# Four projection chunks in one run: moving PSUM users and matmul groups in a fused attention and MoE kernel

## The chip, the cores and the metric

The kernel runs on one core of one Trainium2 chip. The metric is the time of one execution on the device in microseconds; lower is better. Times of a kernel are given as the median of its runs. PE is the tensor engine, PEld its weight loads, DVE the vector engine, ACT the scalar engine, POOL the GpSimd engine, and SP the engine that starts most of the transfers.

## The reference

Eight batches (B = 8) of eight heads, 512 tokens of 64 elements and 32 state rows each. Cross attention goes both ways, and the result of all heads, 512 wide, goes through a two-layer block with an exact Gelu.

```python
scores = scale * np.matmul(x, state.transpose(0, 1, 3, 2))    # softmax over the state rows -> a
xread = np.matmul(a, state)
scores2 = scale * np.matmul(state, x.transpose(0, 1, 3, 2))   # softmax over the tokens -> a2
sread = np.matmul(a2, x)
y = np.concatenate([xread, sread], axis=2)                    # (B, H, 512 + 32, 64)
x = y.transpose(0, 2, 1, 3).reshape(B * 544, 512)
h = x @ w_in                                                  # 512 x 2048
g = 0.5 * h * (1.0 + erf(h / sqrt(2)))
return g @ w_out                                              # 2048 x 512
```

## The kernel before

**The work of a batch.** `scores` (L325) multiplies the transposed tokens with the state and takes the exponential on ACT; `norm` (L347) divides by the row sums on DVE; `atr_dma` (L378) transposes the result into AT by a transfer. The product of attention and first layer is folded: `p_mm` (L423) multiplies the state of a batch with w_in into P, in four chunks f = 0 to 3 of 512 columns. Each chunk is eight matmuls on 64-row, 32-column parts of the PE array, and fills two PSUM banks; `p_copy` (L438) takes the first bank out on ACT and the second on DVE. `mm1` (L489) then makes hidden chunk m of 16 as P times AT, two matmuls of 512 columns into one bank (hp), and ACT's Gelu empties the bank into g. M(k, k + 1) in the text is such a pair of hidden chunks.

**The second layer** goes as seven products of half-size blocks rather than eight, called X with a name "1" to "7" (L621), sixteen matmuls of 256 columns each. Their operands are sums of blocks of g, which `g_sum` (L582) makes on DVE, and of w_out (`w_sums`). X writes one of four fixed banks, o0 to o3: "3" and "5" use o0, "4" and "2" o1, "1" and "7" o2, "6" o3. After "3" ACT copies the bank to s3 (L635); after "4" DVE makes s34 (L640); after "5" ACT copies (L643) and POOL makes u (L646); after "1" DVE makes q (L652); after "2" ACT copies (L648), POOL makes v (L610) and DVE adds v to o3 (L618); after "7" DVE adds u (L654) and SP starts an output transfer.

**The reads.** `sread` (L386) multiplies the exponentials with the tokens on 32-column parts of the array, into one bank; `sread_out` (L400) divides on DVE straight from that bank into srm. `srt` (L413) transposes srm on PE, through another bank, and DVE copies it to XSR (L419).

**PSUM.** There are eight banks: the four fixed ones above, which `otile` gives, and four that `ftile` gives in rotation to scores, hidden chunks, P chunks, reads and srT. A user of a rotating bank waits until the user four before it has been emptied.

**The order** of work on each engine is the program's order, written by hand; no scheduler moves it. The main loop (L1116) has a slot for each batch b from 2 to 7, of eight parts p. A slot runs all hidden chunks of batch b, the X of batch b - 1 (parts 0 to 4) and the X "3" and "6" of batch b, and prepares batch b + 1 (nb): scores in part 1, norms in parts 2 and 3, the transfer of AT in part 5. `p_run` (L898) makes P of nb in two runs of two chunks: in part 5, chunks 0 and 1, after the reads; in part 7, chunks 2 and 3, after the M pair and before X "6". In slot 2, `pmat` (L1142) makes chunks 2 and 3 of batch 2 itself, one each in parts 0 and 3. In slot 6 the reads of batches 6 and 7 are made together. Slot 7 has another body (`read_out_slot`, L923).

Of the kernel before, what the change touches and what calls it, by code (L numbers as in the profile page):

```python
# [9 lines left out]
FP32 = mybir.dt.float32  # L10
BF16 = mybir.dt.bfloat16
# [6 lines left out]
def kernel(  # L18
# [36 lines left out]
    def otile(shape, name, at=None):  # L55
        if at is None:
            at = turn[0] % 4
            turn[0] += 1
        return ps_o.tile(shape, FP32, name=name, tag=f"o{at}")

    def ftile(shape, name):
        return ps_f.tile(shape, FP32, name=name, tag="f")
# [323 lines left out]
    def sread(b):  # L386
        A = atts[b]
        A.sr = ftile([128, 2, 65], "sr")
        for t in range(2):
            for j in range(SJ):  # L390
                for c in range(HC):
                    nc.tensor.matmul(  # L392
                        A.sr[32 * c:32 * c + 32, t, :],
                        lhsT=A.e[:, 2 * j + t, 32 * c:32 * c + 32],
                        rhs=A.xo[:, j, c, 1 + 65 * t:66 + 65 * t],
                        start=(j == 0),
                        stop=(j == SJ - 1),
                    )

    def sread_out(b):  # L400
        A = atts[b]
        A.srm = att.tile([128, 2, D], BF16, name="srm", tag="srm")
        flat = A.sr.rearrange("q t d -> q (t d)")
        inv = att.tile([128, 2], FP32, name="inv", tag="inv")
        nc.vector.reciprocal(out=inv, in_=flat[:, 0:130:129])
        nc.vector.tensor_tensor(
            out=A.srm,
            in0=flat[:, 1:129].rearrange("q (t d) -> q t d", t=2),
            in1=inv[:, :].to_broadcast((128, 2, D)),
            op=ALU.mult,  # L410
        )
# [11 lines left out]
    def p_mm(b, f, tiles):  # L423
        if b not in Ps:
            Ps[b] = att.tile([128, 2, d_ff], BF16, name="P", tag="P")
        ps = [tiles([128, 512], "p_ps") for t in range(2)]
        for c in range(HC):
            for t in range(2):
                nc.tensor.matmul(  # L429
                    ps[t][32 * c:32 * c + 32, :],  # L430
                    lhsT=sbd[64 * t:64 * t + 64, b, c, 32 * t:32 * t + 32],
                    rhs=w_in_bf[64 * t:64 * t + 64, c, f * 512:(f + 1) * 512],
                    start=True,
                    stop=True,
                )
        return ps

    def p_copy(b, f, ps):  # L438
        dst = Ps[b][:, :, f * 512:(f + 1) * 512]
        nc.scalar.copy(out=dst[:, 0, :], in_=ps[0])  # L440
        nc.vector.tensor_copy(out=dst[:, 1, :], in_=ps[1])  # L441

    def pmat(b, f):
        p_copy(b, f, p_mm(b, f, ftile))
# [137 lines left out]
    def g_sum(b, name):  # L582
        (h0, k0), (h1, k1), op = G_SUMS[name]
        t = apool.tile([128, MH, 256], BF16, name="gsum", tag="gsum")
        nc.vector.tensor_tensor(out=t, in0=g_q(b, h0, k0), in1=g_q(b, h1, k1), op=op)  # L585
        xs[b, "g" + name] = t
# [34 lines left out]
    def X(b, name):  # L621
        bank = {"3": 0, "4": 1, "5": 0, "2": 1, "1": 2, "6": 3, "7": 2}[name]
        first = name in "3416"
        if first:
            xs[b, bank] = otile([128, 2, NH], "xp", bank)
        ps = xs[b, bank]
        lhs = {"3": (0, 0), "4": (1, 1)}.get(name)
        lhs = xs[b, "g" + name] if lhs is None else g_q(b, *lhs)
        rhs = {"5": w_q[1][1], "2": w_q[0][0]}.get(name)
        rhs = w_sum[name] if rhs is None else rhs  # L630
        x_mm(ps, lhs, rhs, first)
        if name == "3":
            xs[b, "s3"] = c_tile("s3")
            if b > 1:
                nc.scalar.copy(out=xs[b, "s3"], in_=ps)  # L635
            for h in range(2):
                xs[b, "o", h] = hpool.tile([128, 2, d_model], FP32, name="oh", tag=f"oh{h}")
        elif name == "4":
            xs[b, "s34"] = c_tile("s34")
            nc.vector.tensor_tensor(out=xs[b, "s34"], in0=ps, in1=xs[b, "s3"], op=ALU.add)  # L640
        elif name == "5":
            o = xs[b, "o", 0][:, :, NH:]
            nc.scalar.copy(out=o, in_=ps)  # L643
            xs[b, "u"] = c_tile("u")
            x_out(b, 0, right)
            nc.gpsimd.tensor_tensor(out=xs[b, "u"], in0=xs[b, "s34"], in1=o, op=ALU.subtract)  # L646
        elif name == "2":
            nc.scalar.copy(out=xs[b, "o", 1][:, :, :NH], in_=ps)  # L648
            c22(b)
        elif name == "1":  # L650
            xs[b, "q"] = c_tile("q")
            nc.vector.tensor_tensor(out=xs[b, "q"], in0=ps, in1=xs[b, "s34"], op=ALU.add)  # L652
        elif name == "7":
            nc.vector.tensor_tensor(  # L654
                out=xs[b, "o", 0][:, :, :NH], in0=ps, in1=xs[b, "u"], op=ALU.add
            )
            x_out(b, 0, left)
# [77 lines left out]
    sr = {}  # L735
# [159 lines left out]
            nc.vector.tensor_tensor(out=rs["o", 0][:, :NH], in0=ps, in1=rs["u"], op=add)  # L895
            r_out(0)

    def p_run(b, fs, banks, copy=None):  # L898
        done = []
        for f, at in zip(fs, banks):  # L900
            it = iter(at or ())
            tiles = (lambda shape, name: otile(shape, name, next(it))) if at else ftile
            done.append((b, f, p_mm(b, f, tiles)))
        for x in done:
            (copy or p_copy)(*x)

    def p_copy_v(b, f, ps):
        for t in range(2):
# [6 lines left out]
    def M(*ms):  # L915
        for m in ms:
            mm1(m // MC, m % MC)
# [198 lines left out]
    for b in range(2, B):  # L1116
        nb = b + 1
        for p in range(8):
            k = 16 * b + 2 * p
            if p == 1 and nb < B:  # L1120
                scores(nb, 0)
                scores(nb, 1)
            if p in (2, 3) and nb < B:
                norm(nb, p - 2)
            if p == 3 and nb + 1 < B:
                xtr_dma(nb + 1)
            if p == 5 and nb < B:
                atr_dma(nb)
            if p == 7 and nb < B:
                srt(b)  # L1130
                if nb == B - 1:
                    srt(nb)
            if nb == B and p < 5:
                read_out_slot(p)
                if p == 4:
                    r_homes()
                    r_sum("5")
                    r_sum("2")
                continue
            M(k, k + 1)  # L1140
            if b == 2 and p in (0, 3):
                pmat(2, 2 + p // 3)  # L1142
            if b == 2 and p == 1:
                w_sums(4)
            if p < 5:
                if p == 0:
                    g_sum(b - 1, "5")
                    if b > 2:
                        sr_w("5216"[b - 3])
                X(b - 1, "45127"[p])  # L1150
                if p < 3:
                    g_sum(b - 1, "127"[p])
            if p == 0 and b + 3 < B:
                hold_for(b, 0)
                load_x(4 if b == 2 else b + 3)
            if p == 6 and b == 2:
                hold_for(b, 12)
                load_x(5)
            if p == 0 and nb + 1 < B:
                begin(nb + 1)  # L1160
                rearr(nb + 1)
            if nb == B:
                if p == 5:
                    g_sum(b, "6")
                    R("3")
                    r_sum("1")
                    R("4")
                    r_sum("6")
                    r_sum("7")
                if p == 6:  # L1170
                    R("5")
                    X(b, "3")
                    R("2")
                    R("1")
                if p == 7:
                    R("6")
                    X(b, "6")
                continue
            if p == 5:
                g_sum(b, "6")  # L1180
                reads = (b, nb) if nb == B - 1 else (b,)
                for r in reads:
                    sread(r)
                p_run(nb, (0, 1), ((0, 1), (3, 2)))
                for r in reads:
                    sread_out(r)
                if b == 2:
                    rearr_ones(3)
                elif nb + 1 < B:
                    rearr_ones(nb + 1)  # L1190
            if p == 6:
                X(b, "3")
            if p == 7:
                if b == 2:
                    rearr_ones(4)
                p_run(nb, (2, 3), ((1, 2), None))
                X(b, "6")
    b = B - 1
    for name in "521":
# [39 lines left out]
```

## Time and profile before

| | |
|---|---|
| median of three runs | 203.81 us (203.44 to 204.97) |
| span of the profiled execution | 202.5 us; the page gives no other time of that execution |
| what lies between the span and the runs | 0.9 us to the fastest, 1.3 us to the median |
| slot 2 (first M at 50.85) | 22.24 us |
| slots 3, 4, 5 (first M at 73.09, 94.43, 115.77) | 21.34 us each |
| slot 6 (first M at 137.10, the next slot's at 159.09) | 21.99 us |

The page comes from one execution. Its first part gives the busy time of each engine; matmuls are pipelined, so their durations overlap and the difference of two starts tells what PE spends on a group. A view of the waits says which engine sat idle before which instruction and what ended that. The timeline has one row for each group of like instructions: start, microseconds, engine, line, operation, output and inputs, shape and count, and in square brackets the idle time ahead of it and its releaser.

### The profile page before, as it was taken

How to read it: one execution, taken by the hardware profiler on the slowest of the kernel's cores; microseconds unless marked ns; L12 is line 12 of the kernel's file. 1: busy time of each engine (PE TensorE's matmuls, PEld its weight loads, DVE VectorE, ACT ScalarE, POOL GpSimd, SP SyncE). 2: the span in 40 equal slices, each digit the busy share in tenths (PEclk: the TensorE clock that was granted, in tenths of full speed). 3: DMA queues.
4: the chain of work that ended last, by engine and by line, in shares of the span. 5: the costliest groups of instructions: out<-in, count | busy, mean ns of one | idle time of the engine just before them, and what ended most of it. 6: DMA issues, size and time to landing. Idle time of an engine off the chain costs nothing.

```text
span 202.5 us, 4900 instructions
## 1 busy us (share of the span) xinstructions
PE 196.6 (97%) x2035; PEld 132.6 (65%) x2035; DVE 157.1 (78%) x255; ACT 135.4 (67%) x240; POOL 67.9 (34%) x75
## 2 busy tenths in 40 slices
PE   7898999999999999999999999999999999999994
PEld 2433544465667577766776687567775787878893
DVE  2953776789998979878897787768778988895882
ACT  3785577699885779566967596687847576864120
POOL 8962603323249555360627502430220002200000
PEclk9999999999999999999999999999999999999999
DMA  6999999977675788782774308440107001040125
GB/s 203 174 174 203 205 199 197 181 134 142 96 135 107 207 104 108 155 179 32 90 163 142 77 0 123 130 119 0 52 9 202 3 0 55 0 159 0 52 102 162
DMA packets 40566, 23.16 MB, mean 114 GB/s; under 512 B 21856, under 2 KB 39136, under 8 KB 40544
## 3 DMA queue, kind: packets, MB, share of 16 engines
q0 software_dynamic: 13984, 8.10, 29.3%
q1 hardware_dynamic: 25872, 14.36, 28.5%
q10 hardware_dynamic: 688, 0.39, 0.6%
q8 instruction: 16, 0.26, 0.5%
q14 instruction: 6, 0.05, 0.1%
HBM read 17.30 MB, written 8.91 MB: 129 GB/s over the span
## 4 chain that ended last, share of the span: by engine, by line
PE 89%; DMA 5%; POOL 4%; DVE 0%; issue 0%; POOLq 0%
PE xp L591 41%; PE hp L494 26%; DMA xb<-in_x_dram 5%; PE p_ps L429 4%; PE op L536 4%; PE sp L798 3%; PE rp L864 3%; POOL w_in_bf L105 2%; PE op L520 2%; PE xp L703 2%; PE pt L333 2%; PE sr L392 1%; POOL sbd L95 1%; POOL w_out_bf L113 1%; PE xT_ps L271 1%; POOL st_bf L121 0%
## 5 line engine op out<-in xcount | busy, mean ns | idle before, releaser
L501 ACT ACTIVATE g<-hp 128x512 bf16<-128x512 f32 x124 | 67.1, 605 | 27.9 <-PE hp L494 21.3
L494 PE MATMUL hp<-AT,P 128*128 128x512 bf16 x248 | 62.9, 379 | 0.0
L591 PEld LDWEIGHTS <-gsum 128*128 128x128 bf16 x528 | 51.0, 98 | 12.1 <-issue 1.9
L585 DVE TENSOR_TENSOR gsum<-g 128x2048 bf16<-128x2048 bf16 x35 | 45.5, 1314 | 0.1
L591 PE MATMUL xp<-ws,gsum 128*128 128x256 bf16 x304 | 36.3, 273 | 0.0
L494 PEld LDWEIGHTS <-P 128*128 128x128 bf16 x248 | 22.8, 98 | 20.5 <-issue 2.7
L591 PE MATMUL xp<-ws,g 128*128 128x256 bf16 x224 | 26.8, 273 | 0.0
L591 PE MATMUL xp<-w_out_bf,gsum 128*128 128x256 bf16 x224 | 26.6, 273 | 0.0
L591 PEld LDWEIGHTS <-g 128*128 128x128 bf16 x224 | 21.7, 98 | 4.6 <-issue 0.2
L646 POOL TENSOR_TENSOR u<-s,oh 128x512 f32<-128x512 f32 x6 | 8.8, 1466 | 41.1 <-ACT oh L643 41.1
L441 DVE CAST P<-p_ps 128x512 bf16<-128x512 f32 x29 | 18.7, 683 | 3.1 <-PE p_ps L429 2.9
L440 ACT CAST P<-p_ps 128x512 bf16<-128x512 f32 x29 | 15.8, 599 | 5.4 <-PE p_ps L429 5.1
L225 POOL COPY x<-xb 128x1024 bf16<-128x1024 bf16 x12 | 12.6, 1080 | 15.7 <-DMA xb<-in_x_dram 15.7
L235 POOL COPY xo<-xb 128x1024 bf16<-128x1024 bf16 x12 | 14.5, 1234 | 4.6 <-PE sr L392 4.6
L610 POOL TENSOR_TENSOR v<-q,oh 128x512 f32<-128x512 f32 x6 | 8.6, 1434 | 20.6 <-ACT oh L648 20.5
L536 PE MATMUL op<-w_out_bf,g 128*128 128x512 bf16 x48 | 11.8, 380 | 0.0
L356 DVE TENSOR_TENSOR a<-e,ics 128x512 bf16<-128x512 bf16 x14 | 10.7, 764 | 0.5
L429 PE MATMUL p_ps<-w_in_bf,sbd 64*32 64x512 bf16 x248 | 10.5, 382 | 0.0
L353 DVE TENSOR_REDUCE cs<-e 128x16 f32<-128x512 bf16 x14 | 9.5, 677 | 0.7 <-ACT e L340 0.7
L419 DVE COPY XSR<-srT 128x128 bf16<-128x128 bf16 x8 | 5.7, 759 | 5.5 <-PE srT L416 5.5
L501 ACT ACT_TABLE_LOAD x7 | 9.0, 1283 | 0.1
L618 DVE TENSOR_TENSOR oh<-xp,v 128x512 f32<-128x512 f32 x6 | 4.1, 690 | 5.2 <-POOL v L610 5.2
(132 smaller groups left out, 230.2 us busy)
## 6 DMA issues: line engine op xcount, KB each, us to landing
out_dram<-oh SPq DMA_DIRECT2D x15, 256.0 KB, 2.9
xb<-in_x_dram POOLq DMA_DIRECT2D x7, 512.0 KB, 5.9
out_dram<-oh SPq DMA_DIRECT2D x6, 512.0 KB, 2.9
w_in_bf<-in_moe_w_in_dram POOLq DMA_DIRECT2D x6, 256.0 KB, 12.4
out_dram<-osb SPq DMA_DIRECT2D x5, 256.0 KB, 3.2
w_out_bf<-in_moe_w_out_dram POOLq DMA_DIRECT2D x4, 256.0 KB, 8.9
w_out_bf<-in_moe_w_out_dram POOLq DMA_DIRECT2D x2, 512.0 KB, 13.3
x0f<-in_x_dram SPq DMA_DIRECT2D x3, 256.0 KB, 3.7
```

The lines of the kernel that those rows point to most:

```text
L225: nc.gpsimd.tensor_copy(out=A.x4[:, :, :, 64 * t:64 * t + 64].rearrange("p j c d -> p c j d"), in_=src[:, t],)
L235: eng.tensor_copy(out=A.xo[:, :, :, 2 + 64 * t:66 + 64 * t].rearrange("p j c d -> p c j d"), in_=src[:, t],)
L353: nc.vector.reduce_sum(out=cs, in_=e4, axis=AX.X)
L356: nc.vector.tensor_tensor(out=A.a[:, :, hs].rearrange("p g (c n) -> p g c n", n=NS), in0=e4, in1=ics[:, :, :].to_broadcast((128, G, 2, NS) ...
L429: nc.tensor.matmul(ps[t][32 * c:32 * c + 32, :], lhsT=sbd[64 * t:64 * t + 64, b, c, 32 * t:32 * t + 32], rhs=w_in_bf[64 * t:64 * t + 64, c ...
L440: nc.scalar.copy(out=dst[:, 0, :], in_=ps[0])
L441: nc.vector.tensor_copy(out=dst[:, 1, :], in_=ps[1])
L494: nc.tensor.matmul(hp, lhsT=Ps[b][:, t, m * 128:(m + 1) * 128], rhs=atts[b].AT[:, :, t, :], start=(t == 0), stop=(t == 1),)
L501: nc.scalar.activation(out=gs[b][:, m, :], in_=hp, func=AF.Gelu)
L536: nc.tensor.matmul(ops[b, j], lhsT=gs[b][:, m, j * 128:(j + 1) * 128], rhs=w_out_bf[:, m, :], start=(m == 0), stop=(m == MC - 1),)
L585: nc.vector.tensor_tensor(out=t, in0=g_q(b, h0, k0), in1=g_q(b, h1, k1), op=op)
L591: nc.tensor.matmul(ps[:, j - js[0], :], lhsT=lhs[:, m, 128 * j:128 * j + 128], rhs=rhs[:, m, :], start=(first and j == js[0] and m == 0), ...
```

## The change

In slots 2 to 6 the two runs of two chunks become one run of four in part 5. The run's banks are o0 and a rotating one for chunk 0, two rotating ones for chunk 1, o1 and o3 for chunk 2, o2 and a rotating one for chunk 3. The reads go ahead of it into one rotating bank; ACT copies them to the new tile sraw, and the division (on DVE, after the run's copies) reads sraw. X "7" of batch b - 1 moves from part 4 to part 5, ahead of the reads; X "3" of batch b moves from part 6 to part 5, right behind the run; g_sum "6" moves from part 5 to part 3. Part 4 is left with its M pair alone, part 6 too. In slot 2, chunks 2 and 3 of batch 2 are made as one pair from four rotating banks, in part 2 ahead of X "1", and that part's M pair now follows X "1".

```diff
-    def p_run(b, fs, banks, copy=None):
+    def reads_mm(bs):
+        sr = ftile([128, len(bs), 2, 65], "sr")
...
+        raw = cpool.tile([128, len(bs), 130], FP32, name="sraw", tag="sraw")
+        nc.scalar.copy(out=raw, in_=sr.rearrange("q i t d -> q i (t d)"))
+        return raw
+
+    def reads_norm(bs, raw):
...
+            nc.vector.reciprocal(out=inv, in_=raw[:, i, 0:130:129])
+            nc.vector.tensor_tensor(
+                out=A.srm,
+                in0=raw[:, i, 1:129].rearrange("q (t d) -> q t d", t=2),
+                in1=inv[:, :].to_broadcast((128, 2, D)),
+                op=ALU.mult,
+            )
+
+    def p_all(b, bs):
+        raw = reads_mm(bs)
         done = []
-        for f, at in zip(fs, banks):
...
+        for f, at in enumerate(((0, None), (None, None), (1, 3), (2, None))):
+            it = iter(at)
+
+            def tiles(shape, name):
+                i = next(it)
+                return ftile(shape, name) if i is None else otile(shape, name, i)
+
             done.append((b, f, p_mm(b, f, tiles)))
         for x in done:
-            (copy or p_copy)(*x)
+            p_copy(*x)
+        reads_norm(bs, raw)
+
+    def pmat_pair(b):
+        done = [(b, f, p_mm(b, f, ftile)) for f in (2, 3)]
+        for x in done:
+            p_copy(*x)
...
+            if b == 2 and p == 2:
+                pmat_pair(2)
+                X(1, "1")
+                g_sum(1, "7")
             M(k, k + 1)
-            if b == 2 and p in (0, 3):
-                pmat(2, 2 + p // 3)
...
-            if p < 5:
+            if p < 4 or (p == 4 and nb == B):
...
+                if p == 3:
+                    g_sum(b, "6")
+                if b > 2 or p != 2:
+                    X(b - 1, "45127"[p])
+                    if p < 3:
+                        g_sum(b - 1, "127"[p])
...
             if p == 5:
-                g_sum(b, "6")
+                X(b - 1, "7")
                 reads = (b, nb) if nb == B - 1 else (b,)
-                for r in reads:
-                    sread(r)
-                p_run(nb, (0, 1), ((0, 1), (3, 2)))
-                for r in reads:
-                    sread_out(r)
+                p_all(nb, reads)
...
-            if p == 6:
                 X(b, "3")
             if p == 7:
                 if b == 2:
                     rearr_ones(4)
-                p_run(nb, (2, 3), ((1, 2), None))
                 X(b, "6")
```

More of the change, by code (lines that the diff above doesn't have):

```diff
@@ L896, in R @@
             r_out(0)
-    def p_run(b, fs, banks, copy=None):
-        done = []
-        for f, at in zip(fs, banks):
-            it = iter(at or ())
-            tiles = (lambda shape, name: otile(shape, name, next(it))) if at else ftile
+    def reads_mm(bs):
+        sr = ftile([128, len(bs), 2, 65], "sr")
+        for i, b in enumerate(bs):
+            A = atts[b]
+            for t in range(2):
+                for j in range(SJ):
+                    for c in range(HC):
+                        nc.tensor.matmul(
+                            sr[32 * c:32 * c + 32, i, t, :],
+                            lhsT=A.e[:, 2 * j + t, 32 * c:32 * c + 32],
+                            rhs=A.xo[:, j, c, 1 + 65 * t:66 + 65 * t],
+                            start=(j == 0),
+                            stop=(j == SJ - 1),
+                        )
[3 more added lines that the diff above has]
+    def reads_norm(bs, raw):
+        for i, b in enumerate(bs):
+            A = atts[b]
+            A.srm = att.tile([128, 2, D], BF16, name="srm", tag="srm")
+            inv = att.tile([128, 2], FP32, name="inv", tag="inv")
+            nc.vector.reciprocal(out=inv, in_=raw[:, i, 0:130:129])
[4 more added lines that the diff above has]
+                op=ALU.mult,
+            )
+    def p_all(b, bs):
+        raw = reads_mm(bs)
+        done = []
+        for f, at in enumerate(((0, None), (None, None), (1, 3), (2, None))):
[3 more added lines that the diff above has]
+                return ftile(shape, name) if i is None else otile(shape, name, i)
             done.append((b, f, p_mm(b, f, tiles)))
         for x in done:
-            (copy or p_copy)(*x)
+            p_copy(*x)
[4 more added lines that the diff above has]
+            p_copy(*x)
     def p_copy_v(b, f, ps):
@@ L1149 @@
                         sr_w("5216"[b - 3])
-                X(b - 1, "45127"[p])
-                if p < 3:
-                    g_sum(b - 1, "127"[p])
+                if p == 3:
[4 more added lines that the diff above has]
+                        g_sum(b - 1, "127"[p])
             if p == 0 and b + 3 < B:
```

## The prediction

> **What bounds the kernel now.** I read the totals first, then the waits between 50 and 160 us, then the timeline of the slots that change. The page:
>
> ```profile
> span 202.5 us, 4900 instructions
> ## 1 busy us (share of the span) xinstructions
> PE 196.6 (97%) x2035; PEld 132.6 (65%) x2035; DVE 157.1 (78%) x255; ACT 135.4 (67%) x240; POOL 67.9 (34%) x75
> ```
>
> PE is busy 97% of the span, and its clock row reads 9 in every slice. The waits between 50 and 160 us name no wait of a matmul, only weight loads that waited for "issue". So in slots 2 to 6 time is PE's issue time, and a change there is worth what it takes from PE's stream, less any new wait. PE's rows of the timeline, in the second half of slot 4, which runs from 94.43 to 115.77 (slots 3, 4 and 5 have the same rows, and each lasts 21.34):
>
> ```profile
> 107.95 1.03 PE L494 MATMUL hp<-AT,P 128*128 128x512 bf16 x4
> 108.90 0.43 PE L392 MATMUL sr<-xo,e 128*32 128x65 bf16 x32
> 109.26 0.63 PE L429 MATMUL p_ps<-w_in_bf,sbd 64*32 64x512 bf16 x16
> 109.82 1.04 PE L494 MATMUL hp<-AT,P 128*128 128x512 bf16 x4
> 110.69 1.91 PE L591 MATMUL xp<-ws,g 128*128 128x256 bf16 x16
> 112.44 0.22 PE L416 MATMUL srT<-ident,srm 128*128 128x128 bf16 x1
> 112.50 1.03 PE L494 MATMUL hp<-AT,P 128*128 128x512 bf16 x4
> 113.45 0.62 PE L429 MATMUL p_ps<-w_in_bf,sbd 64*32 64x512 bf16 x16
> 114.01 1.92 PE L591 MATMUL xp<-ws,gsum 128*128 128x256 bf16 x16
> ```
> and ACT's rows of the same stretch:
> ```profile
> 109.73 1.07 ACT L440 CAST P<-p_ps 128x512 bf16<-128x512 f32 x2
> 110.69 1.11 ACT L501 ACTIVATE g<-hp 128x512 bf16<-128x512 f32 x2
> 112.70 0.58 ACT L635 COPY s<-xp 128x512 f32<-128x512 f32 x1 [0.90 <-PE srT L416]
> 113.18 1.09 ACT L501 ACTIVATE g<-hp 128x512 bf16<-128x512 f32 x2
> ```
>
> Columns: start, duration, engine, line. Costs are differences of starts. A run of two chunks takes 0.56 (113.45 to 114.01; 109.26 to 109.82). An M pair (four 512-column matmuls) ahead of a P run takes 0.95 (112.50 to 113.45), ahead of an X 0.86 (97.51 to 98.37 in the same slot): entry costs 0.09. One chunk alone took 0.34 (51.81 to 52.15 in slot 2), so a further chunk adds 0.22 and every run carries 0.12 at its end. X is 1.75, the reads 0.36.
>
> **What is removed.** Slots 2 to 6 lose one run's entry and end each: 0.09 + 0.12 = 0.21, five times 1.05. Slot 2's two single chunks become one pair: 0.21. Slot 6 had a real stall, its second run took 0.88 (156.45 to 157.33) because its last bank waited for the vector copy of the second srT: 0.32 over 0.56. That run's place is gone, so 0.32 more. Sum: 1.58. The number of chunks, matmuls, copies and DMAs stays; added is one ACT copy of the reads per slot. A run of four is not in the trace: I take 0.56 + 2 x 0.22 = 1.00, between 0.91 (four at the bare 512-column step of 0.217 from the M rows, plus the end, rounded) and 1.12 (two runs of two).
>
> The Trainium skill, "TensorEngine Tiling (Array Packing)", Key Properties, says that changing the tiling mode drains the TensorE. The trace has it as the weight loads' idle time of 0.42 at each such change, most of it under matmuls still running; by the rule alone a run fewer could save up to 0.84, by the rows 0.21, and the rows decide.
>
> **What is added: new waits.** Let T be the start of the run of four.
>
> (a) X("3") follows the run directly and writes bank 0, which holds the first chunk. Before, an M pair stood between. ACT starts the first copy at T + 0.47 (109.26 to 109.73; in slot 6 152.20 to 152.67, with ACT idle 0.34 before it); the copy takes 0.585, and PE sees a release some 0.06 later (in slot 6 DVE's copy ended at 156.94 and the waiting chunk started at 156.99): T + 1.12. PE comes at T + 1.00. Wait 0.12. The reads' copy goes ahead of it on ACT: it starts about T + 0.13 (estimate: the last read begins 0.12 ahead of T, and P's copy starts 0.06 after its matmul's modelled end) and must take over 0.34 to delay anything. Its 130 columns aren't in the trace; ACT copies of 128x128 take 0.30 and of 128x256 0.37, so 0 to 0.03; I take 0, and 0.03 in slot 6, which copies 260. Five slots: 0.6 (0 if the drain hides it, 1.0 at 0.2 each).
>
> (b) After X("3") ACT has s3's copy, then the Gelus of chunks 12 and 13. By 110.69, 112.44 and 112.70, s3 starts 0.26 after X's end; the next ACT work starts 0.48 later, a Gelu takes 0.61, the release 0.06: X end + 1.41. The fp32 banks now rotate so that chunk 15 takes chunk 12's bank. PE arrives after an M pair 0.87, srT 0.06 and half a pair 0.43, which is 1.36: wait 0.05, four slots, 0.2. In slot 6 two srT stand in the ring, so chunk 14 takes chunk 12's bank: PE arrives at 0.87 + 0.11 = 0.98, wait 0.43, and chunk 15 another 0.05: 0.48.
>
> (c) The run's last chunk uses bank 2, which X("7") now fills just before. DVE's L654 starts 0.20 after X and takes 0.68; PE gets there 0.09 + 0.36 + 3 x 0.22 = 1.11 after X, so 0.2 to spare. The reads' bank is free earlier. srm now stands behind four vector copies: from L654, 4 x 0.61 and 0.45 put it some 0.3 before srT. Nothing, if DVE isn't late (rival below). On SP, the transposing load of AT goes ahead of X("7")'s output now; AT has about 6 us until it is read, and the output's buffer is written 12 us later. POOL's rearr_ones starts 1.9 later, with no reader before the next slot's reads.
>
> (d) Slot 2 is another matter. The new pair needs four fp32 banks, those of both score tiles and of chunks 2 and 3, while ACT changes tables from Gelu to exponential and back:
>
> ```profile
> 53.13 1.28 ACT L340 ACT_TABLE_LOAD   x1
> 54.42 1.08 ACT L340 ACTIVATE e<-pt 128x512 bf16<-128x512 f32 x2
> 55.52 1.28 ACT L501 ACT_TABLE_LOAD   x1
> 56.82 1.09 ACT L501 ACTIVATE g<-hp 128x512 bf16<-128x512 f32 x2
> ```
> and DVE stands here:
> ```profile
> 58.19 0.68 DVE L353 TENSOR_REDUCE cs<-e 128x16 f32<-128x512 bf16 x1
> 58.90 0.25 DVE L355 RECIPROCAL ics<-cs 128x16 f32<-128x16 f32 x1
> 59.19 1.09 DVE L356 TENSOR_TENSOR a<-e,ics 128x512 bf16<-128x512 bf16 x1
> ```
>
> With slot 2's first chunk gone, X("5"), whose successor starts at 56.98 in the timeline, ends 0.43 sooner (0.34 and an entry), at 56.55, and the pair starts at 56.63. ACT drops one copy (its next work starts 0.49 sooner): Gelus of 2 and 3 start at 56.35 and end at 57.44, free at 57.49. The pair's second chunk was due at 56.86: wait 0.63. Then X("1") 57.82 to 59.57, and chunk 4 (bank copied by ACT, 58.4, in time), but chunk 5 wants the bank that DVE copies. DVE has that copy behind the first norm; its rows move 0.52 earlier (X("4") ends 0.43 sooner, one copy of 0.61 is gone), so the copy starts near 59.7 and frees at 60.4; PE is there at 60.0: wait 0.4. Sum 1.03; 0.5 if DVE keeps up and the pair needs only the first Gelu, 1.6 if both copies are slowed as L356 was (1.09 there against 0.69 elsewhere).
>
> The skill's "ScalarE: Activation LUTs", What ACT_TABLE_LOAD costs, counts 1.28 plus a drain of 1.38 per table switch. By it the pair would wait 1.38 longer and the sum be near 206. The row disagrees: the load began at 55.52 and the Gelu at 56.82.
>
> **Sum.** +0.6 + 0.2 + 0.48 + 1.03 - 1.58 = **+0.7 us**. The page gives the profiled execution's span, 202.5, and no more; it lies 0.9 under the fastest of the three runs and 1.3 under the median of 203.81. The difference holds for both: 203.2 of span, **204.5** as a median.
>
> **Rivals.**
> 1. The saving arrives whole: 203.81 - 1.58 = 202.2, with (a), (b) and (d) hidden. For it: PE never waited between 50 and 160. Against: the table load and both Gelus in (d) are rows, and four banks of a ring of four are wanted at once. With (d) alone: 203.3. Chance of this side, under 203.4: 0.15.
> 2. Slower by more than 1%, through POOL. L618 waits for POOL's v (1.2 each time), and now stands ahead of L654 in front of the run. v took 1.26 to 1.68; (c)'s 0.2 and L618's slack of 0.5 are used up if v takes over about 2.2, as POOL's u did beside DVE's sums (2.23 at 61.15). At 0.4 past that, the last chunk of each run waits 0.4: five times, +2.0, near 206.5. For it: g_sum("6") now runs on DVE beside v. Against: v's rows with sums beside them. Chance 0.12.
> 3. The forecast: 0.73, from 203.4 to 205.8.
>
> **Range.** 203.1 to 205.9: below by (a) and (b) hidden (-0.8) with the runs' spread, above by the upper ends of (a) and (d) (+1.0). A measurement of this kernel tells about 1% from no change. Chances: faster by over 1% 0.03 (the whole saving is 0.8%), within 0.84, slower 0.13.
>
> **What would show it.** In the changed kernel's timeline: a run of four taking 1.0 in slots 3 to 5 and slot lengths within 0.1 of 21.34; X("3") starting 0.06 after ACT's first P copy ends; slot 2's pair taking 1.2 and not 0.56, its second half starting as the Gelu of chunk 3 ends; chunk 5 waiting for DVE. The prediction is wrong if a run of four costs as much as two of two, if the slots lengthen through L654 or L618 ending after the third chunk, or if slot 6's chunk 14 doesn't wait.

## The result

The changed kernel takes 205.16 us (204.47 to 206.04), the kernel before 203.79 (203.31 to 205.23), thirteen runs each. The ratio is 1.006, with a 95% interval of 1.0042 to 1.0079: slower by 0.6%. Forecast were 204.5 and no change of over 1%.

The page of the changed kernel has the span 0.9 us longer, with 0.8 us less of busy PE: what was added is waiting.

```profile
span 203.4 us, 4901 instructions
## 1 busy us (share of the span) xinstructions
PE 195.8 (96%) x2030; PEld 133.9 (66%) x2035; DVE 161.6 (79%) x255; ACT 136.5 (67%) x245; POOL 68.6 (34%) x75
```

The slots tell where. Their lengths are the differences of the starts of their first M pair in the timelines, taken before rounding, and hardly differ from run to run where nothing changes (an untouched slot 3 has 21.34 in each kernel below that leaves it alone). The time ahead of slot 2 does: 50.0 to 53.5 in these profiles, with the same code, and what follows slot 6 varies from 43.4 to 44.1. So a mechanism is read from the slots, and the medians only have to agree.

| slot | before | changed | difference | forecast |
|---|---|---|---|---|
| 2 | 22.24 | 22.67 | +0.43 | +0.78 |
| 3 | 21.34 | 21.68 | +0.34 | -0.04 |
| 4 | 21.34 | 21.74 | +0.40 | -0.04 |
| 5 | 21.34 | 21.25 | -0.09 | -0.04 |
| 6 | 21.98 | 22.03 | +0.05 | +0.10 |
| sum | 108.24 | 109.37 | +1.13 | +0.76 |

(The forecast's column adds the prediction's own terms, slot by slot. Its sum is 0.76 and not the prediction's 0.73, since five waits (a), 0.03 longer in slot 6, make 0.63 and were rounded to 0.6.) Slot 5 is the slot as it was meant. PE's rows of the changed kernel there, and ACT's:

```profile
131.10 1.06 PE L429 MATMUL p_ps<-w_in_bf,sbd 64*32 64x512 bf16 x32
132.21 1.91 PE L591 MATMUL xp<-ws,g 128*128 128x256 bf16 x16
```
```profile
131.33 0.27 ACT L913 COPY sraw<-sr 128x130 f32<-128x130 f32 x1 [1.35 <-PE sr L905]
131.58 2.05 ACT L440 CAST P<-p_ps 128x512 bf16<-128x512 f32 x4
```

From the run to X("3") it is 1.11: 1.00 for four chunks and 0.11 until bank 0 is free. ACT's first copy starts at 131.58, 0.48 after the run, and one such copy takes 0.585: it ends at 132.17, and X follows at 132.21. The reads' copy took 0.27 and was out of the way.

Slot 3's run took 1.53. Here are PE's rows and then DVE's:

```profile
85.48 1.91 PE L591 MATMUL xp<-ws,gsum 128*128 128x256 bf16 x16
87.33 0.43 PE L905 MATMUL sr<-xo,e 128*32 128x65 bf16 x32
87.68 0.99 PE L429 MATMUL p_ps<-w_in_bf,sbd 64*32 64x512 bf16 x24
88.86 0.41 PE L429 MATMUL p_ps<-w_in_bf,sbd 64*32 64x512 bf16 x8 [0.19 <-DVE oh L654]
89.21 1.92 PE L591 MATMUL xp<-ws,g 128*128 128x256 bf16 x16
```
```profile
86.40 1.21 DVE L585 TENSOR_TENSOR gsum<-g 128x2048 bf16<-128x2048 bf16 x1
87.54 0.68 DVE L618 TENSOR_TENSOR oh<-xp,v 128x512 f32<-128x512 f32 x1
88.14 0.67 DVE L654 TENSOR_TENSOR oh<-xp,u 128x512 f32<-128x512 f32 x1
88.74 2.46 DVE L441 CAST P<-p_ps 128x512 bf16<-128x512 f32 x4
```

Three chunks go (x24), the fourth waits for L654, which empties bank 2. X("7") ended at 87.23, so L654 could have begun at 87.43; it began at 88.14, since DVE's queue had g_sum("6") and L618 ahead of it, back to back.

DVE was behind in slot 3 already. With X("3") ahead of the M pair of part 6, the Gelu of chunk 12 runs later, and in slot 2 POOL waits for that Gelu (L954) before it starts a load and then its two copies of `rearr_ones` (L235). These begin at 72.18, and at 70.23 in the kernel before. So they now meet a sum on DVE. The changed kernel's rows, then those of the kernel before:

```profile
72.13 3.16 DVE L585 TENSOR_TENSOR gsum<-g 128x2048 bf16<-128x2048 bf16 x1 [0.99 <-ACT g L501]
72.18 2.03 POOL L235 COPY xo<-xb 128x1024 bf16<-128x1024 bf16 x2
```
```profile
72.49 1.22 DVE L585 TENSOR_TENSOR gsum<-g 128x2048 bf16<-128x2048 bf16 x1
70.23 2.02 POOL L235 COPY xo<-xb 128x1024 bf16<-128x1024 bf16 x2
```

The sum took 3.16 in place of 1.22 and ended 1.08 after the copies. POOL's next work was late too and met DVE again; the second norm of slot 3 ended 13.63 after the slot's start, and 12.28 after it in the kernel before. g_sum("6") came behind that norm. No run isolates POOL's lateness.

Slot 4 shows another form of it, in DVE's rows and POOL's v:

```profile
106.81 2.29 DVE L585 TENSOR_TENSOR gsum<-g 128x2048 bf16<-128x2048 bf16 x1
109.02 0.68 DVE L618 TENSOR_TENSOR oh<-xp,v 128x512 f32<-128x512 f32 x1
109.62 0.67 DVE L654 TENSOR_TENSOR oh<-xp,u 128x512 f32<-128x512 f32 x1
110.22 2.47 DVE L441 CAST P<-p_ps 128x512 bf16<-128x512 f32 x4
112.61 0.15 DVE L921 RECIPROCAL inv<-sraw 128x2 f32<-128x2 f32 x1
112.80 0.75 DVE L922 TENSOR_TENSOR srm<-sraw,inv 128x128 bf16<-128x128 f32 x1
```
```profile
106.34 1.67 POOL L610 TENSOR_TENSOR v<-q,oh 128x512 f32<-128x512 f32 x1 [3.34 <-ACT oh L648]
```

The sum took 2.29 where it took 1.21 in slot 3 and in the kernel before: v had started on POOL 0.47 earlier and ended at 108.01, and the sum lasted 1.09 past that. L654 ended at 110.29, the run took 1.33, and later srm (0.75, and 0.29 in the kernel before) made srT wait 0.29.

Slot 2 has the pair's wait as forecast, but hardly any wait of chunk 5. PE's rows and ACT's:

```profile
54.12 1.91 PE L591 MATMUL xp<-w_out_bf,gsum 128*128 128x256 bf16 x16
55.96 1.25 PE L429 MATMUL p_ps<-w_in_bf,sbd 64*32 64x512 bf16 x16
57.14 1.92 PE L591 MATMUL xp<-ws,gsum 128*128 128x256 bf16 x16
58.90 1.97 PE L494 MATMUL hp<-AT,P 128*128 128x512 bf16 x8
60.70 1.91 PE L591 MATMUL xp<-w_out_bf,gsum 128*128 128x256 bf16 x16
```
```profile
54.37 1.28 ACT L501 ACT_TABLE_LOAD   x1
55.66 1.08 ACT L501 ACTIVATE g<-hp 128x512 bf16<-128x512 f32 x2
```

The pair takes 1.18 and not 0.56: its second half starts at 56.80, just after the second Gelu has ended at 56.74. The eight matmuls of chunks 4 to 7 take 1.80, against 1.73 without a wait. Slot 6, PE's rows:

```profile
155.47 1.03 PE L494 MATMUL hp<-AT,P 128*128 128x512 bf16 x4
156.34 0.36 PE L416 MATMUL srT<-ident,srm 128*128 128x128 bf16 x2
156.87 1.10 PE L494 MATMUL hp<-AT,P 128*128 128x512 bf16 x4 [0.17 <-ACT g L501]
157.81 1.91 PE L591 MATMUL xp<-ws,gsum 128*128 128x256 bf16 x16
```

Chunk 14 starts 0.53 after the two srT, which took 0.11 before: 0.42 of waiting for chunk 12's Gelu.

### The profile page after: what moved, and what is told of

The parts are those of the page before. It is cut to its first block, busy times and chain, and to the rows that moved or that the text cites. A ratio compares the mean times of both kernels' runs of the same rounds, so it can differ in the third digit from the quotient of the medians.

```text
span 203.4 us, 4901 instructions
## 1 busy us (share of the span) xinstructions
PE 195.8 (96%) x2030; PEld 133.9 (66%) x2035; DVE 161.6 (79%) x255; ACT 136.5 (67%) x245; POOL 68.6 (34%) x75
## 4 chain that ended last, share of the span: by engine, by line
PE 71%; DVE 9%; ACT 5%; DMA 5%; POOL 4%; issue 4%; DVEq 0%; ACTq 0%; POOLq 0%
PE xp L591 32%; PE hp L494 21%; DMA xb<-in_x_dram 5%; PE op L536 3%; DVE gsum L585 3%; PE sp L798 3%; PE rp L864 3%; POOL w_in_bf L105 2%; PE op L520 2%; PE xp L703 2%; PE p_ps L429 2%; ACT g L501 2%; DVE P L441 1%; PE pt L333 1%; DVE a L356 1%
## 5 line engine op out<-in xcount | busy, mean ns | idle before, releaser
L501 ACT ACTIVATE g<-hp 128x512 bf16<-128x512 f32 x124 | 66.0, 606 | 21.8 <-PE hp L494 17.2
L494 PE MATMUL hp<-AT,P 128*128 128x512 bf16 x248 | 61.8, 379 | 0.2 <-ACT g L501 0.2
L585 DVE TENSOR_TENSOR gsum<-g 128x2048 bf16<-128x2048 bf16 x35 | 49.6, 1430 | 4.1 <-ACT g L501 4.0
L494 PEld LDWEIGHTS <-P 128*128 128x128 bf16 x248 | 23.3, 98 | 20.5 <-issue 1.8
L225 POOL COPY x<-xb 128x1024 bf16<-128x1024 bf16 x12 | 14.1, 1205 | 16.9 <-DMA xb<-in_x_dram 16.9
L440 ACT CAST P<-p_ps 128x512 bf16<-128x512 f32 x29 | 15.3, 599 | 5.1 <-PE p_ps L429 5.0
L235 POOL COPY xo<-xb 128x1024 bf16<-128x1024 bf16 x12 | 12.2, 1046 | 5.0 <-PE sr L905 5.0
L356 DVE TENSOR_TENSOR a<-e,ics 128x512 bf16<-128x512 bf16 x14 | 11.3, 809 | 0.5
L536 PE MATMUL op<-w_out_bf,g 128*128 128x512 bf16 x44 | 11.1, 380 | 0.5 <-issue 0.3
L954 POOL COPY hold<-g 128x1 bf16<-128x1 bf16 x5 | 2.8, 560 | 16.5 <-ACT g L501 16.5
```

The lines of the kernel that those rows point to most:

```text
L225: nc.gpsimd.tensor_copy(out=A.x4[:, :, :, 64 * t:64 * t + 64].rearrange("p j c d -> p c j d"), in_=src[:, t],)
L235: eng.tensor_copy(out=A.xo[:, :, :, 2 + 64 * t:66 + 64 * t].rearrange("p j c d -> p c j d"), in_=src[:, t],)
L356: nc.vector.tensor_tensor(out=A.a[:, :, hs].rearrange("p g (c n) -> p g c n", n=NS), in0=e4, in1=ics[:, :, :].to_broadcast((128, G, 2, NS) ...
L494: nc.tensor.matmul(hp, lhsT=Ps[b][:, t, m * 128:(m + 1) * 128], rhs=atts[b].AT[:, :, t, :], start=(t == 0), stop=(t == 1),)
L501: nc.scalar.activation(out=gs[b][:, m, :], in_=hp, func=AF.Gelu)
L536: nc.tensor.matmul(ops[b, j], lhsT=gs[b][:, m, j * 128:(j + 1) * 128], rhs=w_out_bf[:, m, :], start=(m == 0), stop=(m == MC - 1),)
```

## The experiments

Two theories stood against each other. W: each merged run saves its 0.21, and the loss is a few waits, each with its own place. R: the run of four, with eight banks to be emptied in one burst, is itself what costs. Slot lengths, in us:

| kernel | 2 | 3 | 4 | 5 | 6 | sum |
|---|---|---|---|---|---|---|
| before | 22.24 | 21.34 | 21.34 | 21.34 | 21.98 | 108.24 |
| changed | 22.67 | 21.68 | 21.74 | 21.25 | 22.03 | 109.37 |
| e1 singles in slot 2 | 22.47 | 21.68 | 21.73 | 21.25 | 22.03 | 109.17 |
| e2 the pair alone | 22.71 | 21.34 | 21.34 | 21.34 | 21.99 | 108.72 |
| e3 g_sum 6 late | 22.67 | 21.25 | 21.95 | 21.25 | 22.88 | 110.01 |
| e4 X 7 in part 4 | 22.75 | 21.68 | 21.74 | 21.38 | 22.03 | 109.58 |
| e5 g_sum 6 early, alone | 22.77 | 22.02 | 22.11 | 21.70 | 22.08 | 110.68 |
| e6 v on DVE | 23.68 | 22.15 | 21.75 | 21.25 | 22.03 | 110.85 |
| e7 the pair later, alone | 22.43 | 21.34 | 21.34 | 21.34 | 21.99 | 108.44 |
| e8 runs of four in three slots | 22.23 | 21.25 | 21.34 | 21.25 | 21.62 | 107.69 |
| e9 the same, with e7's pair | 22.43 | 21.25 | 21.34 | 21.25 | 21.62 | 107.89 |

### e1: the changed kernel with slot 2's single chunks

```diff
-            if b == 2 and p == 2:
-                pmat_pair(2)
-                X(1, "1")
-                g_sum(1, "7")
             M(k, k + 1)
+            if b == 2 and p in (0, 3):
+                pmat(2, 2 + p // 3)
```

> The changed kernel, but batch 2's chunks 2 and 3 stay two single chunks in parts 0 and 3 of slot 2. Theory W (each merged run saves 0.21 us on PE and the loss is a handful of waits that can be named): slot 2 goes from 22.67 to about 22.2, as the pair's wait for the Gelu of chunk 3 (0.62) goes and its saving (0.21) with it; slots 3 to 6 stay at 21.68, 21.74, 21.25 and 22.03. Time about 0.5 under the changed kernel, near 204.6. Rival R (a run of four bursts eight bank copies on ACT and DVE, and every slot pays for it, slot 2 like the others): slot 2 stays near 22.6 and the time at 205.1.

204.92 us; ratio to before 1.0056 (1.0031 to 1.0081). Slot 2 fell by 0.20 and not by 0.5. The pair's wait is gone, but the eight matmuls of chunks 8 to 11 now take 2.00 in place of 1.73: with X("7") moved away they follow each other, and chunk 11 wants the bank of the last single chunk, whose vector copy ends late. A wait of 0.27 had been kept off by X("7"). (The page is of e1's longest execution, 207.76; its first M pair starts only at 53.45, and slots 3 to 6 have the changed kernel's lengths to 0.01.)

### e2: the kernel before with the pair alone

```diff
+            if b == 2 and p == 2:
+                pmat_pair(2)
+                X(1, "1")
+                g_sum(1, "7")
             M(k, k + 1)
-            if b == 2 and p in (0, 3):
-                pmat(2, 2 + p // 3)
```

> The kernel before, with only slot 2's two single chunks put into one pair ahead of X 1. Theory W: the pair waits 0.6 for the Gelu of chunk 3 behind the two table loads, and saves 0.21: slot 2 goes from 22.24 to about 22.7, all other slots stay at 21.34 and 21.99, time up by 0.4 to 0.5. Rival R: a pair of two chunks is no burst of eight banks, so it saves its 0.21: slot 2 at 22.0, time 0.2 down.

204.14 us; ratio 1.0019 (0.9999 to 1.0040). Slot 2 is 22.71, up by 0.47, with the same 1.18 for the pair as in the changed kernel, and the other slots don't move. The pair's place costs this by itself.

### e3: g_sum 6 behind the run

```diff
-                if p == 3:
-                    g_sum(b, "6")
...
                 p_all(nb, reads)
+                g_sum(b, "6")
```

> The changed kernel with g_sum 6 moved from part 3 to behind the run's copies and the reads' division, so that it no longer runs beside POOL's v and no longer stands ahead of L618 and L654 on DVE. Theory W: g_sum 6 takes 1.2 and not 2.3, L654 starts 0.2 after X 7 and the last chunk of the run doesn't wait: slots 3 and 4 fall from 21.68 and 21.74 to 21.25 to 21.45 (X 6 may wait a little for the later sum), time 0.5 to 0.8 under the changed kernel. Rival R: slots 3 and 4 stay near 21.7.

205.76 us; ratio 1.0088 (1.0057 to 1.0118). By the slots it is 0.64 slower than the changed kernel (the two ratios' intervals overlap), where 0.5 to 0.8 faster was expected, though the theory's main reading is there. In slots 3 and 4 the run takes 1.11, and slot 3 is 21.25, although DVE is as late there as before (its second norm ends 13.62 after the slot's start). What was not foreseen are the new waits. DVE's rows of slot 4:

```profile
111.66 0.16 DVE L921 RECIPROCAL inv<-sraw 128x2 f32<-128x2 f32 x1
111.85 1.06 DVE L922 TENSOR_TENSOR srm<-sraw,inv 128x128 bf16<-128x128 f32 x1
112.84 1.21 DVE L585 TENSOR_TENSOR gsum<-g 128x2048 bf16<-128x2048 bf16 x1
```

srm, a piece of 0.29, takes 1.06 since POOL is busy with its two copies of the next batch (110.76 to 112.78) and frees it then; srT waits 0.5. In slot 6 the sum stands ahead of the copies that empty the banks of the two srT. PE's row there:

```profile
157.83 0.59 PE L494 MATMUL hp<-AT,P 128*128 128x512 bf16 x2 [0.77 <-DVE XSR L419]
```

### e4: X 7 back in part 4

```diff
-            if p < 4 or (p == 4 and nb == B):
+            if p < 5:
...
             if p == 5:
-                X(b - 1, "7")
```

> The changed kernel with X 7 back in part 4, ahead of the M pair of part 5; g_sum 6 stays in part 3. Theory W: g_sum 6 still takes 2.3 beside POOL's v and L654 still ends late, but bank 2 has 0.86 more time: the wait inside the run goes from 0.4 and 0.2 to about 0 in slots 3 and 4, whose lengths fall to 21.3 to 21.5 (srT may still wait for srm). Rival R: slots 3 and 4 stay near 21.7, as the burst is the same.

205.10 us; ratio 1.0057 (1.0038 to 1.0077). The expectation failed: slots 3 and 4 kept 21.68 and 21.74, and slot 4's run its 1.33. DVE's rows of slot 4:

```profile
106.95 2.29 DVE L585 TENSOR_TENSOR gsum<-g 128x2048 bf16<-128x2048 bf16 x1
109.16 0.68 DVE L618 TENSOR_TENSOR oh<-xp,v 128x512 f32<-128x512 f32 x1
109.76 0.68 DVE L654 TENSOR_TENSOR oh<-xp,u 128x512 f32<-128x512 f32 x1
```

L654 began at 109.76, though X("7") had ended at 108.19: it waits for its turn behind the sum and L618, not for its operand. So what is late is DVE's queue, and in these two slots moving the matmuls that feed it changes nothing. (In slots 2 and 5 the run took 1.22 and the slots grew by 0.08 and 0.13 over the changed kernel's; why is open.) By itself this run also fits R; e3 (run at 1.11 with the sum elsewhere) and e5 do not.

### e5: the kernel before with g_sum 6 early

```diff
+                if p == 3:
+                    g_sum(b, "6")
                 X(b - 1, "45127"[p])
...
             if p == 5:
-                g_sum(b, "6")
```

> The kernel before, with only g_sum 6 moved from part 5 to part 3 (ahead of X 2), where POOL's v runs beside it. Theory W2 (the sum and POOL's v exclude each other, so the sum takes its own 1.21 and the rest of v, and delays L618 and L654 behind it in DVE's queue): g_sum 6 takes 2.3 in slots 4 to 6, and since the second chunk of the first run also uses banks o3 and o2, that run waits 0.3 to 0.9: slots 3 to 6 grow by that much each, the time by 1.5 to 2.5. Rival (the place of the sum is harmless, the run of four is what costs): slots stay at 21.34 and the time at 203.7.

206.31 us in one run, beside 204.22 for the kernel before. There is no run of four here, and slots 3 to 5 grow by 0.68, 0.77 and 0.36. Slot 6 grows by 0.10, less than was expected, and slot 2 by 0.53, which was not expected: its run waits for L654 too. DVE's rows of slot 4, and PE's:

```profile
107.19 2.29 DVE L585 TENSOR_TENSOR gsum<-g 128x2048 bf16<-128x2048 bf16 x1
109.41 0.68 DVE L618 TENSOR_TENSOR oh<-xp,v 128x512 f32<-128x512 f32 x1
110.01 0.67 DVE L654 TENSOR_TENSOR oh<-xp,u 128x512 f32<-128x512 f32 x1
```
```profile
109.75 0.77 PE L429 MATMUL p_ps<-w_in_bf,sbd 64*32 64x512 bf16 x9
110.73 0.41 PE L429 MATMUL p_ps<-w_in_bf,sbd 64*32 64x512 bf16 x7 [0.22 <-DVE oh L654]
```

The run of two is caught in the same way: one matmul of its second chunk gets through (x9), the next waits for L654. The place of one sum on DVE costs more here (2.44 over the slots) than all the merging was to save (1.58).

### e6: v on DVE

```diff
-        nc.gpsimd.tensor_tensor(
+        nc.vector.tensor_tensor(
             out=xs[b, "v"], in0=xs[b, "q"], in1=o[:, :, :NH], op=ALU.subtract
         )
```

> The changed kernel with v (L610) on DVE instead of POOL, so that nothing of POOL runs beside g_sum 6. Theory W2: g_sum 6 takes 1.2 in every slot; slot 4's run of four falls from 1.33 to 1.11 (L654 ends near 109.8 of the old timeline); slot 3, where DVE is behind already, has v's 0.6 added to its queue and its run stays at 1.5 or grows to 1.9; slots 5 and 6 stay at 21.25 and 22.03. Rival (the run of four's burst): slot 4's run stays at 1.33.

209.23 us in one run (its start alone was 2.1 longer than the changed kernel's, so the slots are what is read). DVE's rows of slot 4:

```profile
110.39 1.22 DVE L585 TENSOR_TENSOR gsum<-g 128x2048 bf16<-128x2048 bf16 x1
111.53 0.68 DVE L610 TENSOR_TENSOR v<-q,oh 128x512 f32<-128x512 f32 x1
112.25 0.69 DVE L618 TENSOR_TENSOR oh<-xp,v 128x512 f32<-128x512 f32 x1
112.86 0.68 DVE L654 TENSOR_TENSOR oh<-xp,u 128x512 f32<-128x512 f32 x1
```

Without POOL's v beside it the sum takes 1.22, in slots 5 and 6 too, and the run of slot 4 takes 1.11, as expected. The slot gains nothing all the same: srm fell beside POOL's copies again (1.08) and srT waited 0.51. Slots 2 and 3, where DVE is behind already, lost 1.0 and 0.5 to the added work; slot 2's loss had not been foreseen.

### e7: the kernel before with the pair later

The pair stands behind X("1") and g_sum("7"), and X("2") comes ahead of the M pair of part 3.

```diff
+            if b == 2 and p == 3:
+                X(1, "2")
             M(k, k + 1)
-            if b == 2 and p in (0, 3):
-                pmat(2, 2 + p // 3)
...
-                X(b - 1, "45127"[p])
-                if p < 3:
-                    g_sum(b - 1, "127"[p])
+                if b > 2 or p != 3:
+                    X(b - 1, "45127"[p])
+                    if p < 3:
+                        g_sum(b - 1, "127"[p])
+                if b == 2 and p == 2:
+                    pmat_pair(2)
```

> The kernel before, with slot 2's two single chunks as one pair behind X 1 and g_sum 7, followed by X 2 and only then the M pair of part 3. By then the four rotating banks have been emptied (the Gelus of chunks 2 to 5 end before X 1 does). Theory W: the pair takes 0.56, nothing waits, the slot saves 0.21 whole: 22.03; time 0.2 down. Rival (a pair costs more than it saves wherever it stands): slot 2 at 22.24 or above.

204.11 us; ratio 0.9989 (0.9972 to 1.0006), which doesn't tell it from before. The pair takes 0.55 and nothing waits near it, but slot 2 is 22.43 and not 22.03. PE's row of the end of that slot:

```profile
69.09 0.23 PE L416 MATMUL srT<-ident,srm 128*128 128x128 bf16 x1 [0.25 <-DVE srm L406]
```

X("3") started at 66.93, so srT was due at 68.68: 0.41 of wait for srm. The pair's two vector copies follow each other ahead of the norm, which then falls beside POOL's v (1.80, and 0.76 in the kernel before); DVE is late to the end of the slot.

### e8 and e9: the run of four where nothing waits for it

Both take the kernel before and give slots 3, 5 and 6 the run of four: slot 3 with the sum behind the run, as in e3, slots 5 and 6 with it in part 3. Slots 2 and 4 keep their two runs. Both srT of slot 6 go to one bank, so the rotation is as in the other slots. e9 adds the pair of e7.

```diff
+    FOUR = (3, 5, 6)
...
+                if p == 3 and b in (5, 6):
+                    g_sum(b, "6")
...
+                if b in FOUR:
+                    X(b - 1, "7")
+                    p_all(nb, reads)
+                    if b == 3:
+                        g_sum(b, "6")
...
+                    X(b, "3")
...
-                srt(b)
-                if nb == B - 1:
-                    srt(nb)
+                srts((b, nb) if nb == B - 1 else (b,))
```

> The kernel before, with the run of four only where no wait was found: slot 3 with g_sum 6 behind the run's copies, slots 5 and 6 with it in part 3; both srT of slot 6 in one bank; slots 2 and 4 with their two runs of two; slot 2's pair as in the run with the pair behind X 1. Theory W: 22.03, 21.25, 21.34, 21.25 and about 21.6, together 107.5 against 108.24 before: 0.7 faster than before, a ratio near 0.9965. Rival (a run of four is no gain in itself): 108.2 or more, no faster than before.

> The fastest version so far without its pair: runs of four in slots 3, 5 and 6, one bank for both srT, and slot 2 exactly as in the kernel before (two single chunks). Theory W: slot 2 goes back from 22.43 to 22.24, the others stay at 21.25, 21.34, 21.25 and 21.62: together 107.7 against 108.24 before and 107.89 with the pair; a ratio to before near 0.9975, if the tail and the start are alike.

e9: 203.44 us beside 204.22 for the kernel before, ratio 0.9961 (0.9942 to 0.9980). e8: 203.30 beside 203.97, ratio 0.9976 (0.9958 to 0.9995). Both are faster than the kernel before; the slots put e8 0.2 ahead of e9, which the intervals can't tell. Slots 3, 5 and 6 came out to 0.02 as expected; slot 2 of e9 was expected at 22.03 and took 22.43, as in e7. In slot 6 of e9 the two srT are followed by chunk 14 after 0.19 and not 0.53. So a run of four is a gain of 0.09 in a slot where only X("3") and chunk 15 wait a little for it, and R falls. Most of the gain of e8, 0.36 of 0.55, is in slot 6, where the run of four also takes away the old stall of 0.32 and both srT share a bank; no run tells these apart. e8 and e9 leave slot 4 alone; a way to have the run there without a wait was not tried.

## Why the prediction was right, and where its steps were not

**The sign and the range** were right: no change of over 1%, a little slower, since waits eat a saving of some 1.6. The size was low, +0.7 forecast, +1.13 measured over the slots and +1.37 between the medians. And of the signs by which the prediction was to be judged, one spoke against it: it called itself wrong "if the slots lengthen through L654 or L618 ending after the third chunk", and slots 3 and 4 did just that.

**The saving.** 0.21 a run was a little low: slot 5 lost 0.09 net with waits of 0.11 and about 0.04 in it, which makes 0.24. The second run's stall of 0.32 in slot 6 went, as said.

**(a) X("3")**: 0.12 forecast, 0.11 measured in slots 5 and 6, 0.16 in slot 2; in slots 3 and 4 it is hidden in the longer wait. The reads' copy, unknown before, took 0.27, and 0.38 in slot 6, and delayed nothing in slot 5.

**(b) Chunks 14 and 15**: 0.48 forecast for slot 6, 0.42 + 0.07 measured; 0.05 in the others, measured 0.04 in slots 2, 3 and 5.

**(c) Bank 2 and srm** is the step that failed: "so 0.2 to spare", "put it some 0.3 before srT", "Nothing, if DVE isn't late". DVE was late, in slots 3 and 4: 0.53 and 0.33 in the run (with (a) in them), 0.29 at srT. The step counted L654 from X("7") and left out what stands ahead of it in DVE's own queue. The second rival named the right place, bank 2 through L618 and L654, and the moved sum, but put the price on v growing over 2.2. In slots 3 and 4 v took 1.27 and 1.67, and the sum grew to 2.29 in slot 4 instead. Only in slot 2 did v grow, to 2.33, and there the run had no such wait: L654 ended at 66.98, just before the last chunk was due at 67.04. The step had also seen that POOL's rearr_ones would start 1.9 later (1.95 in slot 2), but asked only who reads its result, and not which sum on DVE it would then meet.

That price could have been read. In the kernel before a sum took 2.61 beside POOL's copies, and the prediction doesn't use that row:

```profile
97.85 2.61 DVE L585 TENSOR_TENSOR gsum<-g 128x2048 bf16<-128x2048 bf16 x1
97.34 2.02 POOL L225 COPY x<-xb 128x1024 bf16<-128x1024 bf16 x2
```

The runs show the same: 2.29 and 2.31 with v begun first (slots 4 and 5 of the changed kernel, and e5), 1.22 with v taken from POOL (e6). The Trainium skill, "SBUF — State Buffer", section "SBUF: two separate sides", says that VectorE and GpSimd share a pair of SBUF ports under an exclusive lock: a vector operation with two SBUF inputs and a GpSimd operation that reads SBUF don't run together, and the later one waits for the earlier to end. These rows agree with that: in slot 4 the sum lasted 1.09 past the end of v.

The division of srm grew beside POOL as well, to 0.75 in slot 4 of the changed kernel and to 1.06 in e3. Both its inputs are now in SBUF, where L406 read the bank in PSUM. In the kernel before the same division had stood within POOL's copies (109.30 to 112.26) and kept its 0.29:

```profile
111.68 0.29 DVE L406 TENSOR_TENSOR srm<-sr,inv 128x128 bf16<-128x128 f32 x1
109.30 2.96 POOL L235 COPY xo<-xb 128x1024 bf16<-128x1024 bf16 x2 [1.38 <-PE sr L392]
```

e5 has it too, 0.29 at 112.03, within copies from 111.74 to 113.77. So it is the reads' copy out of PSUM, which the change adds, that exposed the division to POOL.

**(d) Slot 2's pair**: forecast 1.2, measured 1.18. Chunk 5's wait was put at 0.4 and measured at 0.07: L356 took 0.69 and not 1.09, since POOL's copies, which had stretched it, began 0.5 after it this time; DVE's copy was done 0.3 earlier than forecast. The drain of 1.38 for each table load, which the Trainium skill gives ("ScalarE: Activation LUTs", section "What ACT_TABLE_LOAD costs"), was not to be seen here either: load at 54.37, Gelu at 55.66.

**The sum** stayed within the range in part by luck: two errors were opposite, 0.35 too much in slot 2, and 0.8 too little in slots 3 and 4. The median moved by 1.37 and the slots by 1.13; the rest lies ahead of slot 2 and behind slot 6, whose lengths differ from one execution to the next, and no run here settles it.

**Smaller slips.** 0.91 as the least time of a run of four isn't what its words give: 4 x 0.217 + 0.12 is 0.99. L618 waited for v by 1.2 in slots 3 to 6, but by 0.56 in slot 2. The weight loads' idle time of 0.42 doesn't stand at each change of tiling: between the reads and the run (109.26) there is none. None of the three bears on the sum. "PE never waited between 50 and 160" doesn't fit the prediction's own stall of 0.32 in slot 6: a wait inside a group of like matmuls lengthens the group's row, and the view of waits did not name it.

## What to carry to other kernels

Where an engine is busy all the time, count a merged group's saving from the starts of its rows, then go through every bank that it takes and follow its releaser's whole queue back, not only the releaser's operand. A vector operation that is moved counts by what POOL does at its new place, and so does POOL's work that a moved group delays. Where slots repeat, their lengths in the profile resolve 0.02 us, and a change can be kept in the slots that it helps.

## What the runs showed that was not expected

- A sum of 1.21 on DVE takes 2.29 to 2.32 if POOL's v has started first, and a division of 0.29 with its inputs in SBUF takes 0.75 to 1.08 behind POOL's copies. A sum that started 0.23 before such copies keeps its 1.21 (87.73 in the kernel before), and POOL's copies take the loss, 2.88 in place of 2.03. The recorded starts don't always tell who is first: at 72.13 a sum recorded 0.05 ahead of POOL's copies took 3.16.
- X("7"), an operation on PE, had kept a wait of 0.27 off chunk 11 (e1); moving it showed a late vector copy that nobody had waited for.
- Moving one sum on DVE by two parts of a slot cost the kernel before 2.4 us over the slots (e5), twice what the whole change cost.
